# Grouped-query attention and a squared-ReLU feed-forward on one core: an earlier key load, a feed-forward opening for the 64-row stretches, and squares on ScalarE

## The chip, the core and the metric

The kernel runs on one core of a Trainium2 chip. A core has a matrix engine (TensorE, "PE" in the profile; its weight loads are a row of their own, "PEld"), three engines for elementwise work (VectorE "DVE", ScalarE "ACT", GpSimd "POOL"), and SyncE ("SP"), which here only issues transfers. Each engine runs its own list of instructions in order; they wait for each other with semaphores. POOL, ACT and SP also issue DMA transfers. SBUF is the working memory; PE writes to PSUM, which has eight banks. The metric is the time of one execution on the device in microseconds, lower is better.

## The reference

For 8 batches of 384 positions, 16 query heads share 4 key/value heads of width 64. The attention output is laid out as 3072 rows of 1024 and goes through a feed-forward block with 2048 hidden units:

```python
scores = scale * np.matmul(q, k.transpose(0, 1, 3, 2))     # scale = 1/8
attn = np.exp(scores - max) / sum                          # softmax over the keys
x = np.matmul(attn, v).transpose(0, 2, 1, 3).reshape(3072, 1024)
h = np.maximum(x @ w_in, 0.0)
out = h * h @ w_out
```

Inputs and output are float32; the kernel multiplies in bf16.

## The kernel before

The program is written through a recorder. `R.add` (class `Recorder`, from line 9) takes an operation, the engine, what it reads and writes, and an estimated cost; it keeps a clock per engine and per DMA ring, and `emit` later writes each engine's list with the semaphore waits that follow from reads and writes. The order of one engine's list is the order in which `R.add` was called for it. A large `while` loop (from line 660) decides that order for PE: at each step it collects candidates with the time at which the estimates say that they could start and a priority, and takes one. So a changed estimate can move instructions without changing any of them.

One batch passes through these steps.

- Loads (POOL's queue): `load_k` (L205) brings 192 KB of keys, `load_q` half of the queries (384 KB), `load_v` the values (192 KB), all turned from float32 into bf16 on the way. Staging tiles are double buffered (`NST = 2`). The weights come once: `w_in` in 8 loads of 512 KB, `w_out` in 4 of 1 MB, by column half `jj` and row half `part` (`load_w_out`, L254). POOL's queue takes them in the order of issue.
- Transposes. `dup_k` copies the keys twice side by side (POOL, L266), `turn_k_dma` (L275) transposes them into `kT`, and `turn_q_dma` (L281) the two halves of the queries into `qT`, both by DMA on SP's queue. For batch 0 and part of batch 1 PE does this. `prepare` puts these jobs into the list `chores`, and the loop does each when the estimate says that its input is there.
- Scores: `burst_small` (L337 on PE). Two heads of width 64 run in the upper and the lower 64 rows of PE at once. ScalarE takes the exponential (L347) out of banks 0 to 3 into `expT`. 12 key blocks make 18 bursts per batch.
- Values: `av` (L363), 8 groups of 18 matmuls with 65 columns (64 values and the row sum). Each group takes one of banks 0 to 5; DVE then takes the reciprocal of the sum (L372) and multiplies (L378) into `o_sb`, which frees the bank. Every second group is followed by a DMA transpose into `xT` on SP's queue (L383).
- Up: 16 tiles of 128 hidden units. At full height `up_part` (L421) runs 8 matmuls of 128 rows per tile. Inside a 64-row stretch `quad` (L458) runs four tiles at once, 64 matmuls of 64 rows, in four phases over banks 4 to 7. DVE applies the ReLU (L471, or L429) into `hr`, a ring of four float32 tiles; the square goes to `h2T`, by ScalarE after a full-height tile (L431), by DVE after a quad (L474).
- Down: `down_part` (L515), groups of four matmuls with 512 columns, 24 groups per batch, in banks 6 and 7; DVE copies each finished bank out (L524), SP stores it (L527). `y_sb` has six slots. Batch 0 needs the second column half of `w_out` from its 13th group on.

The steps of neighbouring batches interleave: while batch b goes through "up", batch b+1's scores are made. The loop has a flag `split`: scores run in 64-row mode, and as long as it is set only scores and quads are taken. In the program before, only a score can set it (L773 to L776). When a batch's scores aren't ready by the estimates, up tiles are taken at full height meanwhile. For batch 2 alone, 3.0 is added to the estimated time of the scores as long as `split` is off (L707). The stretch ends when fewer than four up tiles are left and no score is under way. The loads of batch 2 are issued at the top of the loop (L664 to L670), after all weights.

Of the kernel before, what the change touches and what calls it, by code (L numbers as in the profile page):

```python
# [4 lines left out]
AF = mybir.ActivationFunctionType  # L5
# [3 lines left out]
class Recorder:  # L9
# [35 lines left out]
    def add(self, eng, fn, reads=(), writes=(), dma=None, cost=0.1, issue=0.1, shared=(), after=()):  # L45
        i = len(self.ops)
        deps = self.deps_of(reads, writes)
        raw = {self.writer[r] for r in reads if r in self.writer}
        for r in reads:
            self.readers.setdefault(r, []).append(i)  # L50
        for w in writes:
            self.writer[w] = i
            self.readers[w] = []
        need = set(after)
        for d in deps:
            o = self.ops[d]
            if o["dma"] is None and o["eng"] == eng and dma is None:
                if eng in self.IN_ORDER or d not in raw:
                    continue
            need.add(d)  # L60
        if dma is not None:
            if dma in self.dma_last:
                need.add(self.dma_last[dma])
            self.dma_last[dma] = i
        start = max([self.clock[eng]] + [self.ops[d]["end"] for d in need])
        if dma is not None:
            self.clock[eng] = start + issue
            q = eng
            begin = max(self.ring.get(q, 0.0), start + issue + 0.8)
            if shared and self.ring.get("gpsimd", 0.0) > begin:  # L70
                self.ring["gpsimd"] += shared[1]
                for o in self.ops:
                    if o["eng"] == "gpsimd" and o["dma"] is not None and o["end"] > begin:
                        o["end"] += max(0.0, min(shared[1], o["end"] - 1.2 - begin))
                cost = shared[0]
            self.ring[q] = begin + cost
            end = begin + cost + (1.5 if begin > 30 else 1.2 if eng == "gpsimd" else 0.7)
        else:
            self.clock[eng] = start + cost
            end = start + cost + (0.2 if eng == "tensor" else 0.07)  # L80
        self.ops.append(dict(eng=eng, fn=fn, dma=dma, need=need, signal=False, start=start, end=end))
        return i
# [57 lines left out]
def bass_gqa_attention__then__ffn_squared_relu_kernel(  # L140
# [213 lines left out]
    def av(b, c, banks):  # L354
        g, s2 = c // 2, c % 2
        i = pick(banks)
        po = bank(i)[:, 0:2 * NJ * DP].rearrange("p (f e) -> p f e", f=2 * NJ)

        def mm(pe, f0):
            for f in range(f0, f0 + NJ):  # L360
                for j in range(NJ):
                    w = expT[:, (b * NU + g * NJ + j) % NEX, f % 2, (f // 2) * 128:(f // 2) * 128 + 128]
                    m = pe.matmul(po[:, f - 6 * s2, 0:D + 1], w, v_aug[b % 2][:, g * NJ + j, 0:D + 1],  # L363
                                  start=(j == 0), stop=(j == NJ - 1))
            return m

        R.add("tensor", lambda pe: mm(pe, 6 * s2), reads=av_reads(b, c), writes=[("bank", i)], cost=0.285)
        yield
        R.add("tensor", lambda pe: mm(pe, 6 * s2 + 3), reads=av_reads(b, c), writes=[("bank", i)], cost=0.285)
        r = (b * 8 + c) % 2  # L370
        o = (b * HKV + g) % NO
        R.add("vector", lambda e: e.reciprocal(rinv[r].ap().unsqueeze(2), po[:, :, D:D + 1]),  # L372
              reads=[("bank", i)], writes=[("rinv", r)], cost=0.13)
        rb = rinv[r].ap().unsqueeze(2).to_broadcast([128, 2 * NJ, D])
        dst = o_sb[o][:, s2].rearrange("p (i s) d -> p s i d", s=2)
        srcv = po[:, :, 0:D].rearrange("p (s i) d -> p s i d", s=2)
        rbv = rb.rearrange("p (s i) d -> p s i d", s=2)
        R.add("vector", lambda e: e.tensor_tensor(dst, srcv, rbv, ALU.mult),  # L378
              reads=[("bank", i), ("rinv", r)], writes=[("o_sb", o, s2)], cost=0.48)
# [66 lines left out]
    def quad(b, tiles):  # L446

        rs, ends = [], {}

        def part(phase, k0):  # L450
            xs = ((0, 1), (2, 3), (1, 0), (3, 2))[phase]

            def piece():
                def mm(pe):
                    for kc in range(k0, k0 + 4):
                        for x in range(2):
                            c, r = tiles[xs[x]], slice(64 * x, 64 * x + 64)
                            m = pe.matmul(bank(4 + xs[x])[:, 0:S], w_in_sb[r, kc, c * 128:(c + 1) * 128],  # L458
                                          xT[b % NXT][r, kc, :], start=(phase < 2 and kc == 0),
                                          stop=(phase > 1 and kc == NKC - 1))  # L460
                    return m

                ends[phase] = R.add("tensor", mm, reads=need, writes=[("bank", 4 + i) for i in xs], cost=0.65,
                                    after=(ends[phase - 2],) if phase > 1 and k0 == 0 else ())
                if phase < 2 or k0 == 0:
                    return
                for i in sorted(xs):
                    r = hr_n[0] % NHR
                    hr_n[0] += 1
                    rs.append((tiles[i], r))  # L470
                    R.add("vector", lambda e, r=r, i=i: e.tensor_scalar_max(hr[r][:, :], bank(4 + i)[:, 0:S], 0.0),  # L471
                          reads=[("bank", 4 + i)], writes=[("hr", r)], cost=0.48, after=hr_read.pop(r, ()))
                for c, r in rs if phase == 3 else ():
                    hr_read[r] = (R.add("vector", lambda e, c=c, r=r: e.tensor_tensor(h2T[:, c, :], hr[r][:, :], hr[r][:, :], ALU.mult),  # L474
                          reads=[("hr", r)], writes=[("h2T", c)], cost=0.46),)

            need = [("w_in", tiles[i] * 128 // WC) for i in xs] + [("xT", b % NXT, kc) for kc in range(k0, k0 + 4)]
            return NKC, need, [4 + i for i in xs] if phase < 2 and k0 == 0 else None, piece

        return [part(phase, k0) for phase in range(4) for k0 in (0, 4)]  # L480
# [80 lines left out]
    aug_v(1, "gpsimd")  # L561
    for i in range(6, 8):
        load_w_in(i)
    for jj in range(2):
        for part in range(2):
            load_w_out(jj, part)

    for i in range(2):
        R.add("vector", lambda e, i=i: e.memset(v_aug[i][:, :, D:D + 1], 1.0), writes=[("v_one", i)])
# [90 lines left out]
    while av_q or av_open or sc_q or o_q or lanes or ff["now"] or ff["tiles"] or ff["down"]:  # L660
# [2 lines left out]
        spare = MID if first else tuple(i for i in LOW if i not in held)  # L663
        if loaded + 1 < B and turned >= loaded and not turn_q:  # L664
            loaded += 1
            after = [("qT", (loaded - 1) % 2, HKV - 1, 1)] if loaded > 2 else []
            load_k(loaded, after)
            load_q(loaded, 0, 8)
            load_q(loaded, 8, 16)
            load_v(loaded)  # L670
# [39 lines left out]
        for n, lane in enumerate(lanes):  # L710
            chunks, need, banks, _ = lane[0]
            if x_done[0] >= chunks:
# [3 lines left out]
                        continue  # L716
                    t = max(t, open_bank(banks))
                cand.append((t, 5 + 0.1 * n, n))
        f_head = ff_head(split) if not lanes else None
        if f_head is not None:  # L720
            chunks, need, banks, piece = f_head
            if x_done[ff["b"]] >= chunks:
                t = R.when(reads=need)
                if banks:
                    t = max(t, max(open_bank([i]) for i in banks) if split else open_bank(banks))
                cand.append((t, 5, "ffn"))
        if split and at_edge and len(ff["tiles"]) < 4 and not (sc_q and sc_q[0][1]):
            split = False
# [25 lines left out]
        elif what[2] == "av":  # L754
            b, c = av_q.pop(0)
            av_open = (b, c, av(b, c, spare))
            next(av_open[2])
        elif what[2] == "av2":
            b, c, rest = av_open
            av_open = None  # L760
            next(rest, None)
            pairs += 1
            if b == 0:
                o_q.append((b, c, [("o_sb", (b * HKV + c // 2) % NO, c % 2)]))
            elif c % 2 == 1:
                turn_o_dma(b, c // 2)
                x_done[b] += 2
        elif what[2] == "o":
            b, c, _ = o_q.pop(0)
            turn_o_pe(b, c, spare)  # L770
            x_done[b] += 1
        elif what[2] == "sc":
            b, u = sc_q.pop(0)  # L773
            if b and not split:
                split = True
                R.clock["tensor"] += 0.1  # L776
            burst_small(b, pieces, 2 * (u % 2))
            scored |= tiles
        elif what[2] != "ffn":
            lanes[what[2]].pop(0)[3]()  # L780
            lanes = [x for x in lanes if x]
        else:
            ff_take(split)
    R.add("sync", lambda e: e.nop(), reads=stored)
    R.emit()
# [28 lines left out]
```

The softmax here doesn't subtract the row's maximum and nothing guards it: scores larger than these inputs give would overflow.

## Time and profile before

| | |
|---|---|
| median of 6 runs | 423.73 us (423.14 to 424.91) |
| the profiled execution | 423.16 us, of which the span is 421.2 us |
| PE busy | 415.4 us of the span, granted clock 1.00 |
| DVE, ACT, POOL busy | 198.5, 155.0, 55.4 us |
| DMA | 44.39 MB, mean 105 GB/s; 16 engines nearly full until about 137 us |

Times in the profile are microseconds from the start of the span. "Busy" of an engine is the sum of its instructions. The chain of work that ended last is followed back from the last instruction, at each step to what released it; its shares say what the end waited for. A timeline line gives start, duration, engine, source line and operation, and in brackets the idle time before it with what ended it; "issue" means that the profile shows nothing that the engine waited for. "q" behind an engine is its sequencer, which issues DMAs. PE's matmuls overlap; the distance from one start to the next is what counts.

### The profile page before, as it was taken

Reading aid. Unit: us, or ns where it says so; the run is one execution under the profiler, and the core shown is the slowest. Engines: PE = TensorE matmul, PEld = TensorE weight load, DVE = VectorE, ACT = ScalarE, POOL = GpSimd, SP = SyncE. Lnnn points to the kernel's source line nnn. Section 1 sums busy time; section 2 is a strip of 40 time slices with the busy share of each in tenths; the row PEclk is TensorE's granted clock in tenths of the full one; section 3 lists DMA queues with packets and bytes.
Section 4 is the critical chain, followed back from the end, with each engine's and each line's share of the span. In section 5 each row is a group of like instructions: output and inputs, shape, how many; then the busy total and the mean of one; then the engine's idle time right before and its main releaser. Section 6 shows DMA issues by size and latency. Waiting matters only on the chain.

```text
span 421.2 us, 9496 instructions
## 1 busy us (share of the span) xinstructions
PE 415.4 (99%) x4264; PEld 236.6 (56%) x4264; DVE 198.5 (47%) x432; ACT 155.0 (37%) x178; POOL 55.4 (13%) x68
## 2 busy tenths in 40 slices
PE   8999999998999999999999999999999999999997
PEld 6566744555545674465644666455754567446544
DVE  3664751446414584146821667126751458424312
ACT  6948600287107800186003840058200780003300
POOL 8680001145022000400013000000000000000000
PEclk9999999999999999999999999999999999999999
DMA  9999999999989009930299003910061000520012
GB/s 178 193 180 200 207 183 214 201 142 122 163 202 161 2 10 155 217 74 2 43 222 185 3 2 78 212 51 2 2 126 75 26 2 10 118 82 19 2 71 78
DMA packets 96920, 44.39 MB, mean 105 GB/s; under 512 B 77296, under 2 KB 90864, under 8 KB 96880
## 3 DMA queue, kind: packets, MB, share of 16 engines
q0 software_dynamic: 36544, 17.44, 32.5%
q1 hardware_dynamic: 59664, 25.86, 28.5%
q8 instruction: 33, 0.54, 0.5%
q10 hardware_dynamic: 672, 0.49, 0.4%
q14 instruction: 7, 0.06, 0.0%
HBM read 35.65 MB, written 12.58 MB: 115 GB/s over the span
## 4 chain that ended last, share of the span: by engine, by line
PE 95%; DVE 2%; DMA 1%; ACT 1%; POOL 1%; issue 0%; POOLq 0%
PE ps L515 39%; PE ps L458 31%; PE ps L421 9%; PE ps L363 8%; PE ps L337 7%; DMA q_st<-in_q_dram 1%; DVE h2T L474 1%; ACT expT L347 1%; DVE hr L471 0%; PE ps L311 0%; PE ps L396 0%; DVE o_sb L378 0%; PE ps L294 0%; POOL q_st L239 0%; POOL v_st L232 0%
## 5 line engine op out<-in xcount | busy, mean ns | idle before, releaser
L347 ACT ACTIVATE expT<-ps 128x1024 bf16<-128x1024 f32 (+1 forms) x146 | 138.1, 1017 | 161.1 <-PE ps L337 160.9
L515 PE MATMUL ps<-w_out_sb,h2T 128*128 128x512 bf16 (+2 forms) x784 | 168.2, 375 | 0.0
L458 PE MATMUL ps<-xT,w_in_sb 64*128 64x384 bf16 x1600 | 148.1, 322 | 0.0
L515 PEld LDWEIGHTS ps<-w_out_sb,h2T 128*128 128x128 bf16 x784 | 75.1, 98 | 86.6
L458 PEld LDWEIGHTS ps<-xT,w_in_sb 64*128 64x128 bf16 x1600 | 77.8, 94 | 52.4
L524 DVE COPY y_sb<-ps 128x512 f32<-128x512 f32 (+2 forms) x49 | 33.3, 680 | 112.3 <-PE ps L515 112.3
L471 DVE TENSOR_SCALAR hr<-ps 128x384 f32<-128x384 f32 x100 | 51.1, 553 | 74.1 <-PE ps L458 74.1
L337 PE MATMUL ps<-qT,kT 64*128 64x256 bf16 (+2 forms) x384 | 54.0, 326 | 1.3 <-ACT expT L347 1.1
L474 DVE TENSOR_TENSOR h2T<-hr 128x384 bf16<-128x384 f32 x100 | 48.9, 551 | 0.0
L431 ACT ACTIVATE h2T<-hr 128x384 bf16<-128x384 f32 x28 | 14.6, 522 | 80.7 <-DVE hr L429 80.7
L363 PEld LDWEIGHTS ps<-v_aug,expT 128*128 128x128 bf16 x1152 | 37.2, 98 | 7.6 <-issue 3.0
L363 PE MATMUL ps<-v_aug,expT 128*128 128x65 bf16 x1152 | 40.0, 193 | 1.0 <-issue 0.5
L421 PE MATMUL ps<-xT,w_in_sb 128*128 128x384 bf16 x224 | 37.9, 326 | 0.0
L378 DVE TENSOR_TENSOR o_sb<-ps,rinv 128x384 bf16<-128x384 f32 x64 | 35.7, 558 | 2.2
L421 PEld LDWEIGHTS ps<-xT,w_in_sb 128*128 128x128 bf16 x224 | 21.7, 98 | 14.1 <-issue 0.2
L337 PEld LDWEIGHTS ps<-qT,kT 64*128 64x128 bf16 x384 | 17.4, 94 | 17.1 <-issue 3.2
L429 DVE TENSOR_SCALAR hr<-ps 128x384 f32<-128x384 f32 x28 | 15.5, 557 | 18.6 <-PE ps L421 18.6
L271 POOL COPY v_aug<-v_st 128x768 bf16<-128x768 bf16 x8 | 6.8, 849 | 115.6 <-PE ps L363 90.0
L266 POOL COPY k_dup<-k_st 128x1536 bf16<-128x1536 bf16 x7 | 10.3, 1468 | 40.4 <-DMA k_st<-in_k_dram 40.4
L239 POOL DMA_DIRECT2D q_st<-in_q_dram x17 | 14.8, 886 | 0.9 <-POOLq L799 0.8
L372 DVE RECIPROCAL rinv<-ps 128x6 f32<-128x6 f32 x64 | 12.0, 187 | 6.2 <-PE ps L363 5.9
L207 POOL DMA_DIRECT2D k_st<-in_k_dram x7 | 5.3, 758 | 45.3 <-DMA qT<-q_st 45.3
(27 smaller groups left out, 53.6 us busy)
## 6 DMA issues: line engine op xcount, KB each, us to landing
out_dram<-y_sb SPq DMA_DIRECT2D x47, 256.0 KB, 2.7
q_st<-in_q_dram POOLq DMA_DIRECT2D x14, 384.0 KB, 8.2
w_in_sb<-in_moe_w_in_dram POOLq DMA_DIRECT2D x8, 512.0 KB, 14.7
w_out_sb<-in_moe_w_out_dram POOLq DMA_DIRECT2D x4, 1024.0 KB, 27.8
v_st<-in_v_dram POOLq DMA_DIRECT2D x8, 192.0 KB, 10.0
k_st<-in_k_dram POOLq DMA_DIRECT2D x7, 192.0 KB, 4.7
q_st<-in_q_dram POOLq DMA_DIRECT2D x3, 192.0 KB, 5.2
xT<-o_sb SPq DMA_TRANSPOSE x28, 2.9
```

The costliest lines, as they stand in the source:

```text
L239: R.add("gpsimd", lambda g: g.dma_start(q_st[st][:, h0:h1, :], q[b, h0:h1].rearrange("h (p j) d -> p h (j d)", j=NJ)), writes=[("q_st", st ...
L337: mm = pe.matmul(ps[:, base + x, m * wide:(m + 1) * wide], kT[b % 2][64 * x:64 * x + 64, u, :], q_cols(b, u // NJ, x, c0, c0 + wide))
L347: R.add("scalar", lambda e: e.activation(dst, src, AF.Exp, scale=0.125), reads=keys, writes=[("expT", (b * NU + u) % NEX, t) for u, _, _ i ...
L363: m = pe.matmul(po[:, f - 6 * s2, 0:D + 1], w, v_aug[b % 2][:, g * NJ + j, 0:D + 1], start=(j == 0), stop=(j == NJ - 1))
L378: R.add("vector", lambda e: e.tensor_tensor(dst, srcv, rbv, ALU.mult), reads=[("bank", i), ("rinv", r)], writes=[("o_sb", o, s2)], cost=0.48)
L421: m = pe.matmul(bank(i)[:, 0:S], w_in_sb[:, kc, c * 128:(c + 1) * 128], xT[b % NXT][:, kc, :], start=(kc == 0), stop=(kc == NKC - 1))
L429: R.add("vector", lambda e: e.tensor_scalar_max(hr[r][:, :], bank(i)[:, 0:S], 0.0), reads=[("bank", i)], writes=[("hr", r)], cost=0.48, af ...
L458: m = pe.matmul(bank(4 + xs[x])[:, 0:S], w_in_sb[r, kc, c * 128:(c + 1) * 128], xT[b % NXT][r, kc, :], start=(phase < 2 and kc == 0), stop ...
L471: R.add("vector", lambda e, r=r, i=i: e.tensor_scalar_max(hr[r][:, :], bank(4 + i)[:, 0:S], 0.0), reads=[("bank", 4 + i)], writes=[("hr", ...
L474: hr_read[r] = (R.add("vector", lambda e, c=c, r=r: e.tensor_tensor(h2T[:, c, :], hr[r][:, :], hr[r][:, :], ALU.mult), reads=[("hr", r)], ...
L515: m = pe.matmul(bank(i)[:, 0:n], h2T[:, c, i3 * 128:(i3 + 1) * 128], w_out_sb[:, c, c0:c1], start=(c == 0), stop=(c == NFC - 1))
L524: R.add("vector", lambda e: e.tensor_copy(ysl, bank(i)[:, 0:n]), reads=[("bank", i)], writes=[("y", yb)], cost=0.08 + n / 960)
```

## The change

Five edits.

1. At the top of the loop, batch 2's keys are loaded after the first column half of `w_out` and before the second; queries and values follow the weights as before.
2. A 64-row stretch may begin with a quad: `opening` is true outside a stretch when the next score is a batch's first, the values of the batch before are done and at least four up tiles are left; from batch 2 on the scores must also be expected within 6 us. Choosing the feed-forward then sets `split`.
3. Each of a quad's four squares goes to ScalarE if ScalarE's estimated clock is more than 0.5 us behind PE's.
4. The estimate of the reciprocal (L372) is 0.22 in place of 0.13.
5. The estimate of a DMA transpose that queues behind another beside POOL's loads is 3.0.

```diff
@@ R.add
             begin = max(self.ring.get(q, 0.0), start + issue + 0.8)
+            if shared and begin > start + issue + 0.8:
+                shared = (3.0, shared[1])
             if shared and self.ring.get("gpsimd", 0.0) > begin:
@@ av
         R.add("vector", lambda e: e.reciprocal(rinv[r].ap().unsqueeze(2), po[:, :, D:D + 1]),
-              reads=[("bank", i)], writes=[("rinv", r)], cost=0.13)
+              reads=[("bank", i)], writes=[("rinv", r)], cost=0.22)
@@ quad
                 for c, r in rs if phase == 3 else ():
-                    hr_read[r] = (R.add("vector", lambda e, c=c, r=r: e.tensor_tensor(h2T[:, c, :], hr[r][:, :], hr[r][:, :], ALU.mult),
-                          reads=[("hr", r)], writes=[("h2T", c)], cost=0.46),)
+                    if R.clock["scalar"] < R.clock["tensor"] - 0.5:
+                        R.add("scalar", lambda e, c=c, r=r: e.activation(h2T[:, c, :], hr[r][:, :], AF.Square),
+                              reads=[("hr", r)], writes=[("h2T", c)], cost=0.42)
+                    else:
+                        hr_read[r] = (R.add("vector", lambda e, c=c, r=r: e.tensor_tensor(
+                            h2T[:, c, :], hr[r][:, :], hr[r][:, :], ALU.mult),
+                            reads=[("hr", r)], writes=[("h2T", c)], cost=0.46),)
@@ the first loads
-    for jj in range(2):
-        for part in range(2):
-            load_w_out(jj, part)
+    load_w_out(0, 0)
+    load_w_out(0, 1)
@@ the loop
         if loaded + 1 < B and turned >= loaded and not turn_q:
             loaded += 1
+            if loaded == 2:
+                load_k(2)
+                load_w_out(1, 0)
+                load_w_out(1, 1)
+                load_q(2, 0, 8)
+                load_q(2, 8, 16)
+                load_v(2)
+                continue
...
-        f_head = ff_head(split) if not lanes else None
+        opening = (not split and at_edge and bool(sc_q) and sc_q[0][1] == 0 and sc_q[0][0] == ff["b"] + 1
+                   and pairs >= 8 * sc_q[0][0] and len(ff["tiles"]) >= 4)
+        if opening and sc_q[0][0] > 1:
+            opening = R.when(reads=score_reads(sc_q[0][0], 0)) < now + 6.0
+        f_head = ff_head(split or opening) if not lanes else None
...
-                    t = max(t, max(open_bank([i]) for i in banks) if split else open_bank(banks))
+                    t = max(t, max(open_bank([i]) for i in banks) if split or opening else open_bank(banks))
...
         else:
+            if opening:
+                split = True
+                R.clock["tensor"] += 0.1
             ff_take(split)
```

The lists that result differ as follows. On POOL only the key load has moved. On SP the key transpose of batch 2 goes ahead of the first stores, and its first query transpose follows five stores in place of three. On PE the two column halves of batch 1's feed-forward become: 72 half-height up matmuls, then batch 2's 18 score bursts with the other 184 between them; before, 64 full-height ones came first, and after 128 half-height ones six of the score bursts were left over, among values and downs. Every batch from 1 on now has its values as seven groups, one group of four downs, and the eighth (before: eight in batch 1, a mixture in batch 2, six, downs and two from batch 3 on). One up matmul of batch 0 moves ahead of a transpose near 23 us. Six squares move from DVE to ScalarE: the first of batch 1's first quad, and the first of the last quad inside each of the five periods after it. Source lines of the changed kernel are 2 to 7 higher from the recorder on (L337 becomes L339, L363 L365, L421 L423, L458 L460, L515 L522).

## The prediction

> **What bounds the kernel now.** I read the page's busy shares and its chain first.
>
> ```profile
> span 421.2 us, 9496 instructions
> PE 415.4 (99%) x4264; PEld 236.6 (56%) x4264; DVE 198.5 (47%) x432; ACT 155.0 (37%) x178; POOL 55.4 (13%) x68
> ...
> PE 95%; DVE 2%; DMA 1%; ACT 1%; POOL 1%; issue 0%; POOLq 0%
> ```
>
> PE is the bound nearly throughout, at a granted clock of 1.00, so a change can only win where the matrix engine stands still, and can lose by making it wait. To find where it does, I laid the chain out in order of time.
>
> ```profile
> 29.06 0.54 PE ps L337 x4
> ...
> 127.24 0.54 PE ps L337 x4
> ...
> 146.85 5.20 PE ps L458 x64
> 152.04 3.39 PE ps L363 x108
> 155.44 0.86 PE ps L515 x4
> 156.30 1.09 PE ps L363 x36
> 157.39 19.86 PE ps L515 x92
> 177.25 0.54 PE ps L337 x4
> ```
>
> A batch's period runs from its first score (L337) to the next batch's. From 127.24 on it takes 50.01 us, with no wait in it, and so do the four that follow (177.25, 227.26, 277.30, 327.30, 377.34). The two periods before it, 29.06 to 127.24, take 98.18. They hold two periods' work less the 4 up tiles of batch 0 made before 29 us: 64 half-height matmuls, 5.20 by the 146.85 line. At the steady pace that is 2 x 50.01 - 5.20 = 94.82, so 3.36 us are lost there, and nowhere else after 29 us. The timelines around 52 and 101 us say where.
>
> ```profile
> 51.52 0.56 DVE L378 TENSOR_TENSOR o_sb<-ps,rinv 128x384 bf16<-128x384 f32 x1
> 52.13 1.26 PEld L363 LDWEIGHTS ps<-v_aug,expT 128*128 128x128 bf16 x35 [0.18 <-DVE o_sb L378]
> 54.00 0.20 PE L363 MATMUL ps<-v_aug,expT 128*128 128x65 bf16 x1 [0.48 <-issue]
> ...
> 99.20 1.96 DVE L474 TENSOR_TENSOR h2T<-hr 128x384 bf16<-128x384 f32 x4
> 101.08 0.39 PE L337 MATMUL ps<-qT,kT 64*128 64x256 bf16 x4 [0.91 <-ACT expT L347]
> 101.91 0.72 PE L363 MATMUL ps<-v_aug,expT 128*128 128x65 bf16 x18 [0.44 <-DVE o_sb L378]
> ```
>
> Batch 1's values x probabilities (L363) start at 48.60; the first down matmul comes at 54.04. 144 of them at the 30.5 ns between starts are 4.39, so 1.05 is lost: the 7th group of 18 waits for a PSUM bank until DVE has done four squares and a first output (0.22), the 8th for the second (0.13), and the last matmul for nothing that the trace names (0.65). Batch 2 loses the other 2.31 from 98.37 on: its up tiles run out while four of its twelve key blocks are unscored, and scores, values and downs alternate, waiting for exponentials and DVE. It ran out because 8 up tiles went at full height first (74.93, 10.40 us), waiting for batch 2's keys and queries, whose way is on SP's and POOL's queues:
>
> ```profile
> 65.22 1.47 POOL L266 COPY k_dup<-k_st 128x1536 bf16<-128x1536 bf16 x1 [33.98 <-DMA k_st<-in_k_dram]
> ...
> 64.59 1.56 SPq L527 DMA_DIRECT2D out_dram<-y_sb  x3
> 66.71 5.65 SPq L275 DMA_TRANSPOSE kT<-k_dup  x1
> 72.41 4.01 SPq L281 DMA_TRANSPOSE qT<-q_st  x1
> 76.46 1.05 SPq L527 DMA_DIRECT2D out_dram<-y_sb  x2
> 77.56 3.33 SPq L281 DMA_TRANSPOSE qT<-q_st  x1
> ```
>
> **The change part by part.** No matmul is added or removed; what follows is by the changed program's order on each engine.
>
> Keys. On POOL's queue the loads of w_out land at 45.98, 51.01, 56.09 and 63.33, k at 65.16, the q halves at 68.95 and 73.45, v at 75.86. Moved two places forward, k should land at 51.01 + 1.83 = 52.84 (1.83 is its gap behind its predecessor), the last two w_out parts 1.83 later, at 57.9 and 65.2, the q halves and v unmoved, as no byte is added. In the changed order the 7th value group still starts at 52.14 and takes 0.55, one group of four downs 0.86, the 8th value group 0.55, and the other 92 downs start at 54.10. They need those parts at the 13th and 17th group of four: 54.10 + 11 or 15 x 0.863 = 63.6 and 67.05. Slack 5.7 and 1.9: no cost; if the cover went, each us beyond it would be paid in full. Behind the k_dup copy on POOL stands only v's copy, which waits for 75.86 anyway.
>
> SP. The key transpose follows the fourth xT transpose directly (64.6 instead of 66.71), ahead of three stores; two more stores now stand before the first query transpose. After 5.65 us of issue and five stores of about 0.5 (the fifth's copy done by 71.4) the query transpose issues near 72.7, against 72.41. It landed 5.97 after its issue, the other query transposes up to batch 3's took 4.6 to 7.3, so it lands at 77.3 to 80.0; I take 78.7, by the same half's own row. The second half follows the sixth store, near 77.4, landing about 82.9, and is needed nine score groups later, near 89. Delayed stores cost nothing: six slots hold them, and the first is reused after 100 us.
>
> Opening. The stretch of 64-row work opens with 72 half-height up matmuls at 0.08125 (5.85 us) in place of 64 full ones, then scores, with the other 184 between them. The first score falls at 54.10 + 19.86 + 5.85 = 79.8. My query landing is 1.1 ahead; its bounds give -2.5 to +0.2. I charge 0.1. No score is left over, so batch 2 ends as batch 1 does: all of its 2.31 goes, except a 7th-group wait of 0.22 as in batch 1. Gain 2.09. xT of batch 1, needed at about 74, lands at 71.64.
>
> Reciprocal's planner cost. 0.13 to 0.22 changes no instruction, but the planner now puts one group of four downs after seven value groups, not after six (eight in batch 1). In batch 1 the 0.22 stays; the 8th group's 0.13 goes under those 0.86 us of downs. Of the nameless 0.65 I don't know the cause: if it is tied to a moment (54.00), the downs cover it; if to a place in the instruction stream, it stays, and may come again in batch 2. Bounds +0.65 and -0.65; I take +0.5, since the same place in five steady periods shows none. Gain 0.63. In the prologue one up matmul moves ahead of a transpose of outputs that waited 0.17 at 23.6; the next transpose then waits about 0.12 for its own output: +0.05.
>
> Squares. Where ScalarE is idle, the first of a quad's four squares goes to it: six in all. In the five steady periods the 7th value group now comes at 151.98 + 108 x 0.0305 = 155.27, without downs before it. With four squares the first output is released at 155.68 + 0.05, a wait of 0.46; with three, one DVE step of 0.468 earlier, 155.26. So the edits cancel: 0, bounds 0 and 5 x 0.22 = 1.1 (batch 1's wait each time); I take 0.2. ScalarE's square, 522 ns by the row of 28, lies in its idle 20 us.
>
> The sum: 2.09 + 0.63 + 0.05 - 0.1 - 0.2 = 2.5 us. The profiled execution took 423.16 (421.2 and 1.96 around it), so 420.7; the median of the runs is 0.57 higher: 421.2.
>
> [...]
>
> [...]
>
> **The rivals.** (1) Waits remain that I let go: the 0.65 stays in batch 1 and comes again in batch 2, or the steady periods wait 0.2 each. Takes 0.6 to 1.6 from the gain: about 422.2. For it: the 0.65 has no named cause; the margin of 155.26 to 155.27 is nothing.
> (2) Slower: batch 2's queries come late. The first score now has 5.85 us of cover behind the downs instead of 10.40, and PE works in order, so each us after 79.8 is paid in full. If POOL's load is what holds SP, the key transpose's issue ends when it did before, at 72.36, though it starts 2.1 earlier; after five stores the query transpose issues at 74.9, and with the 10.4 that the key transpose took to land it is there at 85.3. A wait of 5.5 against my other gains of 2.6 gives 423.73 + 2.9 = 426.6; it is slower by over 0.85 from a landing at 83.3 on. Against it: POOL's queue is empty at 75.9, before most of that transpose.
> (3) Nothing measurable: a landing near 82 is a wait of 2.2 and leaves 0.4 of gain: 423.3.
>
> **How the numbers follow.** 0.2% of 423.73 is 0.85 us, about what a measurement of this kernel can tell from no change. Forecast 0.57 (all bounds at their best give 2.09 + 0.78 + 0.17 = 3.0, so its own range is 420.7 to 421.8), rival 1 0.25, rival 2 0.08, rival 3 0.10. All of the forecast and of rival 1 lie under 423.73 - 0.85 = 422.88. Faster 0.82, same 0.10, slower 0.08. The range takes both, and 0.3 below the best for the spread of the runs: 420.4 to 422.7.
>
> **What would show it.** In the changed profile: first score of batch 2 at 79 to 80 with no wait for qT or kT; its scores (L339) over before its values; no ACT wait after 98; first score of batch 3 near 124.5 instead of 127.24; steady periods still 50.0; the key copy at about 53 on POOL; 34 squares on ScalarE of 522 ns, 94 on DVE. I am wrong if a period from batch 3 on grows, if the last w_out part lands after 67, if PE waits at the first score for a DMA, or if a wait put down to "issue" appears among the values of batches 1 and 2.

## The result and the profile after

The changed kernel takes 421.96 us (median of 22 runs, 421.48 to 423.57) against 423.61 us for the kernel before beside it (48 runs): a ratio of 0.9961, 95% interval 0.9953 to 0.997. That is 1.65 us less; the forecast was 421.2 us, 0.8 us lower. The profiled execution took 421.89 us. These are the busy shares and the chain of its page:

```profile
span 419.9 us, 9623 instructions
PE 414.8 (99%) x4328; PEld 236.8 (56%) x4328; DVE 200.1 (48%) x434; ACT 154.2 (37%) x176; POOL 55.4 (13%) x68
...
PE 92%; DMA 3%; DVE 2%; ACT 1%; POOL 1%; issue 0%; SPq 0%; POOLq 0%
```

PE is still the bound, but the chain now goes through a transfer (DMA 3% instead of 1%, and SP's queue is new in it). The chain of the changed kernel in order of time (start, duration, group) shows which:

```profile
29.26 0.54 PE ps L339 x4
...
52.34 0.72 PE ps L365 x18
53.06 0.86 PE ps L522 x4
53.92 0.40 PE ps L365 x13
54.56 0.33 PE ps L365 x5
54.89 16.42 PE ps L522 x76
71.33 0.70 DVE y_sb L531
72.03 0.37 SPq L534
72.44 0.44 SPq L534
72.93 0.55 SPq L534
73.53 7.84 DMA qT<-q_st
81.42 0.61 PE ps L339 x4
...
125.90 0.54 PE ps L339 x4
...
175.92 0.54 PE ps L339 x4
```

The two periods from batch 1's first score to batch 3's take 125.90 - 29.26 = 96.64 us, 1.54 less than before (98.18). The next period takes 50.02 (before 50.01). Ahead of 29 us another 0.15 is gained: the first score comes 20.22 after the landing of batch 0's second query load, before 20.37. Together 1.69, close to the 1.65 between the medians. So the gain is in the two periods where it was expected, and it is 1 us smaller there than the prediction's terms.

In the chain the downs of 54.89 to 71.33 now lead to a copy on DVE, the issue of three stores on SP, the transpose of batch 2's first queries, and only then to batch 2's first score. The timeline of PE (start, duration, and in brackets the idle time with its releaser) has two waits in the first of the two periods:

```profile
54.56 0.33 PE L365 MATMUL ps<-v_aug,expT 128*128 128x65 bf16 x5 [0.24 <-issue]
...
81.42 0.61 PE L339 MATMUL ps<-qT,kT 64*128 64x512 bf16 x4 [0.72 <-DMA qT<-q_st]
```

Measured between starts of matmuls, the first is 0.40 us: the wait that the profile puts down to nothing is still there, smaller than its 0.65 before. The second is new: the last up matmul starts at 80.38, and the score starts 1.04 later; every other score burst that follows a half-height up matmul in this trace starts 0.16 later, so 0.88 are lost. The queue of SP shows the way of those queries:

```profile
60.36 5.04 SPq L385 DMA_TRANSPOSE xT<-o_sb  x1
65.44 5.36 SPq L277 DMA_TRANSPOSE kT<-k_dup  x1
70.85 2.63 SPq L534 DMA_DIRECT2D out_dram<-y_sb  x5
73.53 3.04 SPq L283 DMA_TRANSPOSE qT<-q_st  x1
76.61 0.57 SPq L534 DMA_DIRECT2D out_dram<-y_sb  x1
77.23 3.42 SPq L283 DMA_TRANSPOSE qT<-q_st  x1
```

At the steady pace the two periods would take 94.82 us, as worked out before the change. Most of the losses above it can now be named one by one, each taken from the distances between starts on PE:

| us lost in the two periods | before | after |
|---|---|---|
| above 94.82 in all | 3.36 | 1.82 |
| 7th value group waits for a bank, batch 1 | 0.22 | 0.22 |
| the same, batch 2 | in the 2.31 | 0.24 |
| 8th value group, batch 1 | 0.13 | none |
| wait without a name near 54 | 0.65 | 0.40 |
| batch 2's scores left over among values and downs | 2.31 | none |
| first score of batch 2 waits for its queries | none | 0.88 |

The rows for "before" add up to 3.31 of the 3.36, those for "after" to 1.74 of the 1.82.

### The profile page after: what moved, and what is told of

It reads as the page before. It is cut to its first block, busy times and chain, and to the rows that moved or that the text cites. A ratio compares the mean times of both kernels' runs of the same rounds, so it can differ in the third digit from the quotient of the medians.

```text
span 419.9 us, 9623 instructions
## 1 busy us (share of the span) xinstructions
PE 414.8 (99%) x4328; PEld 236.8 (56%) x4328; DVE 200.1 (48%) x434; ACT 154.2 (37%) x176; POOL 55.4 (13%) x68
## 4 chain that ended last, share of the span: by engine, by line
PE 92%; DMA 3%; DVE 2%; ACT 1%; POOL 1%; issue 0%; SPq 0%; POOLq 0%
PE ps L522 39%; PE ps L460 32%; PE ps L339 7%; PE ps L365 7%; PE ps L423 6%; DMA qT<-q_st 2%; DMA q_st<-in_q_dram 1%; DVE h2T L480 1%; ACT expT L349 1%; DVE hr L473 0%; PE ps L313 0%; PE ps L398 0%; SPq L534 0%; DVE o_sb L380 0%; DVE y_sb L531 0%
## 5 line engine op out<-in xcount | busy, mean ns | idle before, releaser
L522 PE MATMUL ps<-w_out_sb,h2T 128*128 128x512 bf16 (+2 forms) x784 | 168.2, 375 | 0.0
L460 PE MATMUL ps<-xT,w_in_sb 64*128 64x384 bf16 x1728 | 159.7, 323 | 0.0
L522 PEld LDWEIGHTS ps<-w_out_sb,h2T 128*128 128x128 bf16 x784 | 75.1, 98 | 86.6
L460 PEld LDWEIGHTS ps<-xT,w_in_sb 64*128 64x128 bf16 x1728 | 84.0, 94 | 56.8 <-issue 0.4
L339 PE MATMUL ps<-qT,kT 64*128 64x256 bf16 (+2 forms) x384 | 54.3, 326 | 1.0 <-DMA qT<-q_st 0.7
L480 DVE TENSOR_TENSOR h2T<-hr 128x384 bf16<-128x384 f32 x102 | 51.2, 563 | 0.0
L365 PEld LDWEIGHTS ps<-v_aug,expT 128*128 128x128 bf16 x1152 | 37.1, 98 | 6.3 <-issue 1.4
L365 PE MATMUL ps<-v_aug,expT 128*128 128x65 bf16 x1152 | 39.7, 193 | 0.4 <-issue 0.2
L423 PE MATMUL ps<-xT,w_in_sb 128*128 128x384 bf16 x160 | 27.3, 326 | 0.0
L339 PEld LDWEIGHTS ps<-qT,kT 64*128 64x128 bf16 x384 | 17.7, 94 | 16.3 <-issue 2.4
L433 ACT ACTIVATE h2T<-hr 128x384 bf16<-128x384 f32 x20 | 10.4, 522 | 44.1 <-DVE hr L431 44.0
L423 PEld LDWEIGHTS ps<-xT,w_in_sb 128*128 128x128 bf16 x160 | 15.4, 98 | 9.8 <-issue 0.2
L477 ACT ACTIVATE h2T<-hr 128x384 bf16<-128x384 f32 x6 | 3.1, 523 | 46.6 <-DVE hr L473 46.6
```

The source lines that it names most:

```text
L339: mm = pe.matmul(ps[:, base + x, m * wide:(m + 1) * wide], kT[b % 2][64 * x:64 * x + 64, u, :], q_cols(b, u // NJ, x, c0, c0 + wide))
L423: m = pe.matmul(bank(i)[:, 0:S], w_in_sb[:, kc, c * 128:(c + 1) * 128], xT[b % NXT][:, kc, :], start=(kc == 0), stop=(kc == NKC - 1))
L522: m = pe.matmul(bank(i)[:, 0:n], h2T[:, c, i3 * 128:(i3 + 1) * 128], w_out_sb[:, c, c0:c1], start=(c == 0), stop=(c == NFC - 1))
```

## The experiments

Every edit below is to the changed kernel ("..." leaves lines out). The two traces suggest that the opening brings its 2.09, but that the first score of batch 2 is now set by SP's chain of key transpose, five stores and query transpose, so that whatever PE saves ahead of it is swallowed there. Each expectation sets two or three theories (A, B, C) against each other and says anew what they stand for. Each run has its own kernel before beside it, with medians of 423.63 to 423.72.

### Each edit undone

**The opening.** The flag never becomes true, so a stretch begins with a score again.

```diff
-                   and pairs >= 8 * sc_q[0][0] and len(ff["tiles"]) >= 4)
+                   and pairs >= 8 * sc_q[0][0] and len(ff["tiles"]) >= 4) and False
```

> The changed kernel without edit 2: a stretch can begin with a score only; keys, squares and estimates stay changed. In its order batch 1's up work runs 56 half-height matmuls' worth at full height first, and five of the 18 score bursts of batch 2 are left for the time of the values. Theory A (the gain is that all scores of batch 2 fit into the stretch): the left-over scores again meet ScalarE and DVE at the end of the stretch, 1.0 to 2.0 us of the loss of 2.31 come back, part of it offset because the first score, at full height, doesn't wait for the queries: 422.6 to 423.6. Theory B (the gain comes from the keys and from the values' new grouping, and the opening only rearranges): within 0.3 of the changed kernel's 421.96.

Measured: 422.78 us (11 runs), ratio 0.9987 (0.9978 to 0.9996). The two periods take 97.47, the query transpose lands at 81.85 and the first score comes at 83.04 with no wait for it, but the leftover scores are back, as PE's timeline of this kernel shows:

```profile
97.35 0.61 PE L339 MATMUL ps<-qT,kT 64*128 64x512 bf16 x4
98.86 0.39 PE L339 MATMUL ps<-qT,kT 64*128 64x256 bf16 x4 [0.91 <-ACT expT L349]
99.69 0.72 PE L365 MATMUL ps<-v_aug,expT 128*128 128x65 bf16 x18 [0.43 <-DVE o_sb L380]
```

Without the opening PE waits there for exponentials and for DVE (1.28 and 0.70 us between starts); with it those waits are gone and 0.88 comes back as the wait for the queries. The opening is worth 0.8 us in this kernel, not 2.09, mainly for that reason; the wait without a name near 54 us is also 0.24 shorter without the opening.

**The key load.** Back to its old place, behind all of `w_out`.

```diff
             if loaded == 2:
-                load_k(2)
                 load_w_out(1, 0)
                 load_w_out(1, 1)
+                load_k(2)
```

> The changed kernel without edit 1: batch 2's keys load after all of w_out, and the recorder's estimates then put four stores ahead of the key transpose on SP and both query transposes behind the fifth. The opening has 56 half-height matmuls. Theory A (what last released the first score was the first query transpose on SP's queue, which landed at 81.37): the key transpose waits for the fourth store and issues near 71 instead of 65.4, the query transpose near 75 to 76 instead of 73.5; it lands near 82.5 and the first score, due at about 79.2, waits about 3 us instead of 0.8; 423.5 to 424.5. Theory B (the keys' place is worth nothing, since the queries came last in either order): 421.8 to 422.3.

Measured: 424.43 us (median of 11 runs, of which the profiled one took 1530.8), ratio 1.0019 (1.0007 to 1.003) from the ten others. Five of them, with a mean granted clock of 1.00, take 423.55 to 423.98, level with the kernel before (423.60 at that clock); the other five, at 0.996, take 424.43 to 425.29. So the gain over the kernel before is gone; that this kernel is slower than that one rests on the five runs at 0.996. The same program was run once more for a trace that can be read beside the others.

> The same program as the one without the key move, for a profile that can be read (the first one's execution was disturbed). Its time was 424.43, between the 423.5 and 424.5 of theory A, so: the key transpose issues near 71 on SP, the first query transpose near 75 to 76, landing near 82.5; PE's first score of batch 2, due near 79.2, waits 3 us for it. If instead the first score waits for the key transpose, or the time went to the end of the stretch, theory A had the right sum for a wrong reason.

Measured: 424.04 us in that one run; the two periods take 98.79. SP's queue of this kernel:

```profile
64.97 5.62 SPq L534 DMA_DIRECT2D out_dram<-y_sb  x4
70.64 1.61 SPq L277 DMA_TRANSPOSE kT<-k_dup  x1
72.30 1.37 SPq L534 DMA_DIRECT2D out_dram<-y_sb  x1
73.71 6.24 SPq L283 DMA_TRANSPOSE qT<-q_st  x2
```

The queries are issued at 73.71, hardly later than with the early keys (73.53) and earlier than expected, and land at 81.65; but the planner puts 56 up matmuls instead of 72 behind the downs, so PE comes to the first score earlier and loses 2.52 us until 81.70. A second loss came with it, in batch 2's values. These are lines of DVE, POOL and PE from the timelines of the same kernel:

```profile
103.00 3.23 DVE L480 TENSOR_TENSOR h2T<-hr 128x384 bf16<-128x384 f32 x4
```

```profile
103.08 1.80 POOL L268 COPY k_dup<-k_st 128x1536 bf16<-128x1536 bf16 x1 [0.26 <-DMA k_st<-in_k_dram]
```

```profile
105.25 1.02 PE L522 MATMUL ps<-w_out_sb,h2T 128*128 128x512 bf16 x4
106.98 1.42 PE L365 MATMUL ps<-v_aug,expT 128*128 128x65 bf16 x36 [0.70 <-DVE o_sb L380]
```

Four squares, 1.96 us elsewhere, take 3.23: a key copy runs beside them, one square takes 1.82 instead of 0.55, and the 7th value group comes 0.86 us later than without a wait. So the earlier keys matter by the order that the planner makes with them, more than by when the keys themselves are there. In this trace the longer wait for the queries (2.52 - 0.88 = 1.64), the collision (0.86 instead of the 0.24 at that group) and 0.13 at the eighth group, which follows without downs here, less 0.25 by which the nameless wait is shorter, make 2.14, against the 2.15 us that the two periods are longer than in the changed kernel.

**The squares.** Every square of a quad on DVE again (the planner then also puts the four downs two value groups earlier in the steady periods).

```diff
-                    if R.clock["scalar"] < R.clock["tensor"] - 0.5:
+                    if False:
```

> The changed kernel without edit 3: all four squares of a quad stay on DVE; the recorder answers by putting the downs after the sixth value group in the five steady periods, as before the change. Theory A (squares and grouping cancel: a steady period was 50.01 us before and is 50.02 now, without waits in both): 421.96 within 0.2. Theory B (relief of DVE is part of the gain): slower by five times 0.1 to 0.46, 422.5 to 424.2.

Measured: 421.69 us (5 runs), ratio 0.9962 (0.9949 to 0.9974), two periods 96.71, a steady period 50.02. The squares on ScalarE are worth nothing that can be measured.

**The reciprocal's estimate.** Back to 0.13.

```diff
-              reads=[("bank", i)], writes=[("rinv", r)], cost=0.22)
+              reads=[("bank", i)], writes=[("rinv", r)], cost=0.13)
```

> The changed kernel without edit 4: the reciprocal's estimate is 0.13 again, and all eight value groups of every batch stand in one row with no downs between them. Theory A (the downs between cover the eighth group's wait, which is one DVE step of 0.694 against 0.55 of value matmuls): 0.12 to 0.16 in each of seven batches, 1.0 us, and in batch 1 the nameless wait before the 727th matmul grows from 0.40 back to about 0.65: 423.0 to 423.4. Theory B (the grouping is worth nothing because DVE keeps up): 421.96 within 0.2.

Measured: 423.19 us (11 runs), ratio 0.9988 (0.9975 to 1.0); two periods 97.55, a steady period 50.16. PE's timeline of this kernel near 54 us:

```profile
49.84 3.54 PE L365 MATMUL ps<-v_aug,expT 128*128 128x65 bf16 x98
54.12 0.20 PE L365 MATMUL ps<-v_aug,expT 128*128 128x65 bf16 x1 [0.74 <-issue]
```

With the old estimate all eight value groups of batch 1 come in a row, and the nameless wait is 0.90 us (with the four downs between: 0.40). From batch 2's first score on each period loses about 0.14, 0.89 us to the end; that is the eighth group's wait. The other 0.76 us of this trace lies ahead of that score, where PE waits 1.00 us for the queries: they land 52.95 us after batch 1's first score, in the changed kernel 52.18. Whether that later landing comes from the estimate is open. By the medians the estimate, which changes no instruction, is worth 1.2 us through the order that it gives.

### The queries first

If SP's order is the bound, the first query transpose ahead of the five stores must give the loss back. The list of operations is permuted after planning, so that nothing changes on any other engine; `ahead` moves one recorded DMA right behind another:

```diff
+    def ahead(name, of):
+        ops = R.ops
+        i = next(n for n, o in enumerate(ops) if o["dma"] == name)
+        j = next(n for n, o in enumerate(ops) if o["dma"] == of) + 1
...
+        order = list(range(j)) + [i] + list(range(j, i)) + list(range(i + 1, len(ops)))
...
+    ahead("turn_q0", "turn_k")
     R.add("sync", lambda e: e.nop(), reads=stored)
```

> The changed kernel with one instruction moved on SP: batch 2's first query transpose is issued directly after the key transpose, ahead of the five stores; every other engine's order is the same. Its input landed at 68.83 and the key transpose's issue ended at 70.81, so it issues at 70.9 instead of 73.53. Theory A (the first score's wait of 0.8 is owed to the five stores ahead of the queries on SP): it lands near 77 to 79, before the first score at 80.5; the wait is gone and the time is 421.1 to 421.3. Theory B (transposes land at the pace of the DMA engines, behind POOL's load, and an earlier issue changes nothing): landing stays at 80 to 81.4, 421.6 to 422.0. Theory C (stores now collide with the second query transpose): the second half lands after 89 and the 10th score burst waits; slower than 421.96.

Measured: 420.74 us (5 runs, 420.5 to 421.09), ratio 0.9929 (0.9917 to 0.9941). SP's queue, then PE's timeline, of this kernel:

```profile
65.61 5.36 SPq L277 DMA_TRANSPOSE kT<-k_dup  x1
71.02 3.85 SPq L283 DMA_TRANSPOSE qT<-q_st  x1
74.91 4.41 SPq L534 DMA_DIRECT2D out_dram<-y_sb  x6
79.36 1.49 SPq L283 DMA_TRANSPOSE qT<-q_st  x1
```

```profile
75.77 5.04 PE L460 MATMUL ps<-xT,w_in_sb 64*128 64x384 bf16 x60
80.64 0.59 PE L339 MATMUL ps<-qT,kT 64*128 64x512 bf16 x4
```

The transpose is issued 2.5 us earlier and lands 4.4 us earlier, at 76.94; the score follows its predecessor without a wait. The two periods take 95.75, 0.89 less than in the changed kernel, nearly all of it the 0.88 of the wait. The loss was a matter of SP's order alone. Above the steady 94.82 there remain 0.93 us, of which 0.85 are named: 0.23 and 0.24 at the seventh groups and 0.38 for the wait without a name.

### The wait without a name

It stands between the 727th and the 728th matmul on PE's list, both before and after, though the time and the work around it differ (54.00 and 54.56 us; without and with downs before it). To move the place against the work, ten of the 27 warm-up matmuls at the start are left out.

```diff
-    warm_up(27, 2.77)
+    warm_up(17, 2.77)
```

> The changed kernel with 17 instead of 27 warm-up matmuls at the start, so that PE's instruction list is ten matmuls and ten weight loads shorter ahead of everything else; the warm-ups' product is not used. Theory A (the wait of 0.65 before and 0.40 after stands at one place in PE's instruction list: before the 727th matmul in both traces, with a 16 KB transfer of the instruction queue that ended 1.3 to 1.5 us earlier): the wait now falls ten matmuls later in the work, among the downs, where PE takes 0.216 per matmul, and is gone or under 0.1: 421.5 to 421.7. Theory B (it is tied to the moment, the DMA load around 54 us): it stays at 0.4 near 54.5 us: 421.96 within 0.15. Theory C (a shorter warm-up lowers the granted clock at the start): the first microseconds slow down, over 422.2.

Measured: 422.49 us (12 runs), ratio 0.9972 (0.9962 to 0.9981): the wait is gone and the two periods take 95.96, yet the kernel isn't faster than the changed one; the wait is as theory A has it, the time as theory C, whose lower clock this trace doesn't show (it has no record of the clock). In its profiled execution the first score of batch 1 comes at 29.72, which is 21.01 us after batch 0's second query load lands (changed kernel 20.22): PE's matmuls step from 107 to 56 ns apart only at about 9.7 us, against 6.6 in the changed kernel. That late step doesn't follow from the number of warm-ups alone: the next program, which has both edits, steps near 7.0 us with the same 17, and its first score comes 20.22 after that landing. Why the median of these 12 runs is 0.5 us above the changed kernel's stays open, the more as the profiled execution took 421.77.

> The query transpose ahead of the stores and ten fewer warm-ups together. If both waits are separate and both theories A hold, the gains add: 421.96 - 0.8 - 0.35 = 420.8, and the two periods from batch 1's first score to batch 3's take 95.4 to 95.6 us instead of 96.64. If one wait only hides the other, as when PE comes earlier to a score whose queries come no earlier, the sum is smaller: 421.1 to 421.5.

Measured: 420.67 us (5 runs), ratio 0.9929 (0.9915 to 0.9942), two periods 95.34, first scores at 28.82, 79.75 and 124.15. This is level with the queries first alone. To shorten the list without less warming up, 13 warm-up matmuls of 256 columns take the place of 27 of 128.

```diff
-    warm_up(27, 2.77)
+    wide = nc.const_aps.tensor(1.0, (128, 256), bf16)
...
+        for _ in range(13):
+            m = pe.matmul(bank(7)[:, 0:256], ones, wide)
...
```

> The changed kernel with its first 27 warm-up matmuls of 128 columns replaced by 13 of 256, the same 2.8 us of work (their product is not used) in 14 fewer matmuls and weight loads. With ten fewer warm-ups the wait before the 727th matmul was gone (the two periods took 95.96 instead of 96.64), but the first score of batch 1 came at 29.72 instead of 29.19, because PE's pace stepped from 107 to 56 ns per matmul only at 9.7 us instead of 6.6. Theory A (the place in the instruction list alone matters, and the step comes early again with PE kept busy): two periods 96.0 to 96.3, the first score of batch 1 20.2 after the landing of the queries it follows, and 421.5 to 421.7. Theory B (the time without the wait comes from something else in that run): the wait is back near 54.5 us, and 421.96 within 0.15.

Measured: 421.95 us (6 runs), ratio 0.9965 (0.9953 to 0.9978); the two periods take 96.68, as in the changed kernel (96.64). PE's timeline of this kernel at the first score:

```profile
75.83 4.06 PE L460 MATMUL ps<-xT,w_in_sb 64*128 64x384 bf16 x48
81.07 0.61 PE L339 MATMUL ps<-qT,kT 64*128 64x512 bf16 x4 [1.18 <-DMA qT<-q_st]
```

The nameless wait is gone, PE comes to the score earlier and waits 1.34 us instead of 0.88 for queries that land when they did (52.22 us after batch 1's first score, against 52.18). The two waits lie in series, and the second swallows what the first gives. With the queries first there is nothing left to swallow it:

> The wide warm-ups together with the query transpose ahead of the stores. Theory A: both waits gone, two periods 95.3 to 95.4 as with ten fewer warm-ups, 420.3 to 420.5 against 420.74 for the query transpose alone. Theory B (the instruction wait is hidden by something else once the queries come early): 420.74 within 0.15.

Measured: 420.50 us (5 runs, 420.33 to 420.78), ratio 0.9926 (0.9913 to 0.9939). The two periods take 95.44, the first scores come at 29.00, 80.04 and 124.44. PE's timeline of this kernel where the wait was:

```profile
52.81 1.03 PE L522 MATMUL ps<-w_out_sb,h2T 128*128 128x512 bf16 x4
53.68 0.71 PE L365 MATMUL ps<-v_aug,expT 128*128 128x65 bf16 x18
54.23 2.97 PE L522 MATMUL ps<-w_out_sb,h2T 128*128 128x512 bf16 x13
```

Eighteen matmuls of the eighth group in 0.55 us, and the downs behind them. This kernel is faster than both others: 3.1 us under the one before beside it, against 1.65 for the change itself. Of the two additions the order on SP is the larger; the warm-ups' 0.24 us lies within the spread of the runs, and only the two periods (95.44 against 95.75) speak for it.

## Why the prediction was right, and where it was off

The sign and the place were right, and the time lies inside the range; the forecast missed by 0.8 us. The range held because it also took in rival 1: 421.96 is outside the forecast's own 420.7 to 421.8, and the larger part of the shortfall came by another way than rival 1's. Two of the prediction's four signs of being wrong appeared, PE's wait for a DMA at the first score and a wait put down to "issue" among batch 1's values. Term by term the traces give 2.07 (opening) + 0.38 (reciprocal) + 0.15 (prologue) - 0.88 (queries) and nothing for the squares, 1.72 in place of 2.5; the 0.3 us by which the prologue and the squares were better than forecast hide part of the error. Point by point:

- **Opening, 2.09.** The mechanism is as described: batch 2 has no score left over, no wait for ScalarE after 98 us, and the second period (from the first matmul's start at 81.42 to the one at 125.83, 44.41 us) is 50.01 less the 5.85 of up matmuls done before it, plus the seventh group's wait (0.24), within 0.01. Without the opening the waits are back (97.47). With the queries first, the two periods gain 2.43 of the 2.62 that the prediction's terms give for them (2.09 + 0.63 - 0.1), and with the wide warm-ups 2.74.
- **The step that failed: "I take 78.7, by the same half's own row".** The queries landed at 81.37. Of the 2.7 us, 0.8 is the issue, at 73.53 instead of 72.7: the fourth xT transpose began 0.2 later and kept SP 5.04 us where 4.40 before, so the key transpose started at 65.44 instead of 64.6. The other 1.9 is the flight. The 5.97 us that I took belonged to a transpose issued directly behind the key transpose; this one is issued behind five stores, which land ahead of it, and took 7.84. Even my upper bound, 80.0, was too low, since its 7.3 came from transposes elsewhere. The row had the right operation and the wrong neighbours. The 0.1 charged for it measured 0.88, and rival 2's mechanism (queries late behind the stores) is there at a sixth of its size.
- **What followed from it: 0.38 of the reciprocal's 0.63, gained ahead of batch 2's first score, could not shorten the time.** It lies before a point that a transfer sets. The wide warm-ups show it: 0.4 us saved at 54 us, and the two periods stay at 96.68. The prediction added such gains as if PE alone set the time.
- **Reciprocal, 0.63.** The eighth group's 0.13 went under the downs as predicted. Of the nameless 0.65, I let 0.5 go, arguing from a moment in time; 0.25 went, and it is tied to the place in PE's list, which was the other alternative named there. That part of rival 1 came true in batch 1 and not in batch 2.
- **Squares, -0.2.** Nothing: the steady periods are 50.02 with them and without them. The row of 522 ns was right (523 here). Each of the two traces has one table load in the whole run, 1.283 us at 1.75, though squares and exponentials take turns on ScalarE: 12 of the 28 squares before and 9 of the 26 after lie between exponentials, and all took 522 to 523 ns. The counts weren't: 102 squares on DVE and 26 on ScalarE instead of 94 and 34, since I left out that the eight tiles that became quads take their squares from ScalarE back to DVE.
- **Keys.** The loads landed as worked out: keys at 52.455 (52.84 predicted), the two `w_out` parts at 57.69 and 65.13 (57.9 and 65.2), and no down waited. The copy ran after batch 1's squares, as these lines of POOL's timeline and of DVE's, of the changed kernel, show:

```profile
52.51 1.47 POOL L268 COPY k_dup<-k_st 128x1536 bf16<-128x1536 bf16 x1 [21.05 <-DMA k_st<-in_k_dram]
```

```profile
49.63 1.96 DVE L480 TENSOR_TENSOR h2T<-hr 128x384 bf16<-128x384 f32 x4
```

- **Prologue, 0.05.** 0.15 measured, near its bound of 0.17; executions differ by as much there (20.22 us from that landing to the first score in the changed kernel, 20.52 and 20.53 in two of the runs above).
- **"No matmul is added or removed."** The changed kernel has 64 more (4328 against 4264), since batch 1's first eight up tiles go from 64 full-height matmuls to 128 half-height ones; at 0.1625 and 0.08125 us from start to start the work is the same, and nothing in the sum rests on it.

## What to carry to other kernels

When a change gives an in-order engine less work ahead of a transfer's landing, follow the queue that issues that transfer in its new order, and count its landing from the landings of what stands in front of it, not from the flight that the same operation had elsewhere. An estimate from the kernel before (its key transpose landed 10.4 us after its issue, two stores 0.64 apart, the query transpose 1.3 behind the keys) gives 64.6 + 10.4 + 5 x 0.64 + 1.3 = 79.5, nearer than 78.7 and still 1.9 early; so a margin of 1 us between such a landing and its consumer is too thin to count on. Gains ahead of a point that a transfer sets don't add to gains behind it (with the wide warm-ups 0.40 us less at 54 us left the two periods at 96.68 against 96.64): ask first which of the two chains arrives last. And when the transfer is late, look whether something that nobody waits for (here five stores with free slots) stands in front of it; moving it behind was worth 0.9 us in the two periods here, 1.2 between the medians.

## What the runs showed that was not expected

**On SP's queue a transfer landed behind all that were issued before it.** In each of the eleven traces that can be read, the 98 transfers that SP issued landed in the order of their issue. In the changed kernel the key transpose landed at 75.35, the five stores at 76.00, 76.60, 77.19, 77.86 and 78.59, and the first query transpose at 81.37. From the start of its issue to its landing this transpose took 5.9 to 6.2 us in the four programs where it stands directly behind the key transpose (landing 1.3 to 1.4 after it), and 7.5 to 8.5 us in the seven where a store stands directly ahead. So the 7.84 us of the changed kernel are 1.82 until the keys land, 3.24 for the five stores and 2.78 more; the 5.97 before are 4.69 until the keys land and 1.28 more. Why 2.78 pass behind the last store is open: the second query transpose landed 1.15 to 1.5 us behind its predecessor in all eleven programs, in ten of them behind a store. So a store directly ahead doesn't lengthen a flight at every time. The stores were not tried on another queue.

**One wait belonged to a place in the instruction list.** Between PE's 727th and 728th matmul 0.15 to 0.90 us go by with nothing that the profile waits for, in the kernel before, in the changed one, and in those with one edit undone (0.15 without the early keys, 0.90 without the reciprocal's estimate); with a list shorter by 10 or 14 matmuls ahead of that point the wait is gone. An instruction transfer of 16 KB on queue 8 ends 1.3 to 1.5 us before PE goes on (begun 51.68 before, 52.11 after, 0.96 to 0.98 long). That PE waits for its instructions there is an argument from these times, not shown.

**PE's pace at the start steps where the trace's record of the granted clock begins.** The matmuls' spacing goes from 107 to 56 ns at 6.6 us in the changed kernel. Every view gives a granted clock of 1.00 for the time before as well, but the trace file has its first record of the clock only from 6.53 us on. Seven of the traces have such a record, beginning between 4.68 and 6.95 us, and in each the step comes within 0.2 us of it; the others, that of the step at 9.7 us among them, have none. So the 1.00 ahead of the step is not a measurement. The number of warm-ups doesn't fix the step: with 27 of them it came between 4.0 and 6.6 us, with 17 near 7.0 in one program and at 9.7 in the other.

**A square on VectorE took up to three times as long beside a copy on GpSimd.** In the changed kernel the values' copy starts at 95.48 and a square beside it takes 1.18 us instead of 0.55, off the path; in the kernel without the early keys a key copy at 103.08 makes one take 1.82, and PE pays 0.86. In both the copy began while the square before was running (95.17 to 95.72; 103.00 to 103.55), and the next square began while the copy ran and ended 0.4 us after its end. In the kernel before, the values' copy at 94.36 came into a running square too (94.10 to 94.65, 553 ns), but that was the quad's last, and DVE's next instruction began at 96.74, after the copy's end at 95.34. In all three the square that was running kept its 0.55 us, and the copy took longer than elsewhere: 929 and 977 ns for the values' where the seven others in each trace took 827 to 842, 1.80 us for the keys' where those of the two traces took 1.47. Whether the order of the two starts decides which of them waits, as these three suggest, no run tried.

**The runs with the queries first lie closer together.** Those of each of the three kernels lie within 0.63 us of each other (5 runs each); those of the changed kernel span 2.1 us (22 runs), those of the kernel before 2.6 (48 runs). Fewer runs span less, and a part of the kernel before's spread goes with the granted clock: of its runs beside the experiments, 52 with a mean of 1.00 lie between 423.05 and 424.26, and two at 0.996 took 425.32 and 425.61 (two far outliers left out). Whether the order on SP makes the rest is not shown; the kernel before doesn't wait for its queries in the trace either.
